# Sparse attention and an FFN on one core: x written by quarters, first-layer matmuls in halves at the block ends, more places for the first attention groups, named PSUM banks, new planner durations

## The chip, the cores and the metric

The kernel runs on one core of one Trainium2 chip. The time is the device time of one execution in microseconds (us); the kernel before has a median of 849.59 us over three runs (847.49 to 852.67). One execution was profiled.

The engines are called as the profile calls them: PE is the matmul engine (PEld its weight loads), DVE the vector engine, ACT the scalar engine, POOL the GpSimd engine, SP the engine that issues nearly all DMAs. PSUM is the memory that matmuls write to, SBUF the memory that all engines read.

## The reference

Attention over 8 batches of 8 heads, 576 tokens and 64 columns a head, followed by a two-layer feed-forward net on the 4608 resulting tokens:

```python
scores = q @ k.T / sqrt(64)            # per batch and head
mask_local   = (rel >= 0) & (rel < 32)               # heads 0 to 3; rel = query - key position
mask_strided = (rel >= 0) & (key % 32 == query % 32) # heads 4 to 7
attn = softmax(where(mask, scores, -1e9))
x = (attn @ v), heads side by side     # 4608 x 512
h = x @ w_in                           # 512 x 2048
out = (h * sigmoid(h)) @ w_out         # 2048 x 512
```

All is float32. The matmul operands of the net are split into a high part and a low part (`fp32r`), and each product is made of three matmuls: high by high, high by low, low by high.

## The kernel before, in words

**Attention.** Only the allowed pairs of queries and keys are computed. A batch is cut into six groups, three of local heads and three of strided heads; batch 0 runs group by group (units 0 to 5), the other batches in units of two groups (units 6 and up). A unit c passes these steps: `k` (DMA of queries and keys into one of three buffers `kd`), `S` (scores, PE, into a PSUM double bank), `M` (mask and row maximum, DVE, one pair of instructions per 128x64 piece), then for the first nine units `U` (subtraction on POOL) and `E` (one wide exponential on ACT), for later units one exponential with an accumulated sum per piece (`E c.j`, ACT), `R` (row sums and reciprocals, DVE), `N` (scaling, DVE), `T` (transposes, PE), `P` (copy from PSUM to a place `pt`, ACT), `v` (DMA of values), `O` (PE) and `B` (copy into `x`, ACT). In batch 0 the scores use the one double bank `pa`; transposes and `O` use the two double banks `po`.

**The net.** Tokens are worked in blocks of 512. Blocks 0 to 2 run directly: for each of 16 slices fc of the hidden width, the first layer is 12 matmuls 128x512 (`hidden`, L556 to L566; in block 0 as two halves `h` and `i` of six), then `t` (tanh, ACT), `g` (gate, DVE L577), `w` and `l` (high and low part of the result, DVE or ACT), then `o` (second layer, 12 matmuls, L610). A PSUM bank `ph` is given back by `g`; there are two. The weights are loaded in 32 pieces during block 0: `p` (DMA), `a` (two ACT instructions), `j` (DVE L333), `b` (high part, ACT or DVE), `d` (low part, DVE L373). The input of a block is split by `H` (high part, `x_high`, L551) and `L` (low part, `x_low`, L555), a step for each quarter cc of 128 columns of x; quarters 0 and 1 need the local heads, 2 and 3 the strided ones. The six remaining blocks run in three pairs with seven products in place of eight (steps `A`, L1325, and `B`, L1363; operands split by `hi` and `lo`; results by `rs` and stored by `st`). Meanwhile POOL forms sums of weights (`whole`, `sums`) for the pairs.

**The order.** Nothing is ordered by hand. Each step is an object of the class `Steps` with engines and costs, a due time, the steps that it follows and the rings of buffers that it takes from. `arrange` keeps a clock for each engine, picks among the steps that can start within `SOON` (0.05 us) of the earliest the one that is due first, and emits its instructions. Every engine then executes its own list strictly in that order, with waits on semaphores. So each changed cost, ring or dependence changes the lists of all engines.

**What the steps below touch.** In block 0 and in the step from block 0 to block 1, `x` is two tiles `xhi` and `xlo`; those of block 1 are new tiles in the same place, so that each of the eight steps `H1` and `L1` follows the last first-layer matmul of block 0, and the first matmul of block 1 follows all of them.

Of the kernel before, what the change touches and what calls it, by code (L numbers as in the profile page):

```python
# [106 lines left out]
SOON = 0.05  # L107

# [9 lines left out]
class Steps:  # L118
# [72 lines left out]
    def arrange(self):  # L191
# [18 lines left out]
        while len(order) < len(self.all):  # L210
# [11 lines left out]
            soon = [c for c in could if c[0] <= now + SOON]  # L222
# [18 lines left out]
def sparse_attention_ffn(ctx: ExitStack, tc: tile.TileContext, kqt, vt, w_in, w_out, out, out_t):  # L241
# [156 lines left out]
    class Attention:  # L398


        def __init__(self, b, gis):
# [71 lines left out]
        def scale(self):  # L473
            nc.vector.tensor_mul(self.s_sb, self.s_sb, self.inv)
# [8 lines left out]
        def turned(self, i):  # L483
            if i == 0:
                self.pt = att.tile([P, 7 * P], F32, name="pt", bufs=1)
            c0, n = self.c0[i] * P, self.gs[i].n * P
            nc.scalar.copy(out=self.pt[:, c0 : c0 + n], in_=self.psp[:, i, :n])
# [65 lines left out]
    def x_low(k, x, cc):  # L553
        for src, to in parts(k, cc):
            nc.vector.tensor_sub(out=x[1][:, cc, to], in0=src, in1=x[0][:, cc, to].bitcast(F32))  # L555
# [85 lines left out]
    def add_scores(c, t0=None):  # L641
# [4 lines left out]
        for g, gi, k in zip(a.gs, a.gis, a.k):  # L646
# [3 lines left out]
        s = do(f"S{c}", {"PE": 0.3 + sum(0.3 if g.local else 0.4 for g in a.gs)}, a.scores,  # L650
               reads=[f"kd{k}" for k in a.k], writes=[f"pss{c}"], takes=["pa"], due=after(0))
        ms = []
        for i, g in enumerate(a.gs):
# [931 lines left out]
```

## Time and profile before

| what | value |
|---|---|
| median of three runs | 849.59 us |
| profiled execution: its own time | 846.44 us |
| profiled execution: span from first to last instruction | 844.7 us |
| PE busy | 820.5 us (97%) |
| DVE, ACT, POOL busy | 529.5, 462.5, 117.6 us |
| DMA | 180.99 MB, mean 214 GB/s |

The time outside of the span is 1.74 us. The page's first part gives busy times, its second the span in 40 slices, its fourth the chain of waits that ended last; the timeline lists each engine's instructions in order of time with the idle time before them and what ended it in brackets; the view of stretches adds up each engine's busy time between given times.

### The profile page before, as it was taken

To read this page: it belongs to the slowest core of one execution; us is meant where nothing else is said; L and a number is where in the kernel's file an instruction comes from. 1 tells how busy PE (TensorE), PEld (TensorE's weight loads), DVE (VectorE), ACT (ScalarE), POOL (GpSimd) and SP (SyncE) were. 2 spreads that over 40 slices of the span, in tenths; PEclk is the share of its full clock that TensorE was granted. 3 is DMA by queue.
4 is the path that set the end of the run, shared out by engine and by line. 5 is a ranking of instruction groups with operands and counts; after the bars stand their busy time and mean duration, and the time that the engine had idled before them with its cause. 6 is when DMAs were issued, how large, how long until landed. Compare 5 with 4: busy or idle time off the path is not lost.

```text
span 844.7 us, 17679 instructions
## 1 busy us (share of the span) xinstructions
PE 820.5 (97%) x7040; PEld 669.1 (79%) x7040; DVE 529.5 (63%) x1257; ACT 462.5 (55%) x1051; POOL 117.6 (14%) x130
## 2 busy tenths in 40 slices
PE   5799998999999999999999999999999999999997
PEld 4588886788878888788888878888888888888886
DVE  5899777665575667712598675333886460289662
ACT  3888566545355545657596654565444344454440
POOL 4100003553563553000000000000000000000000
PEclk9999999999999999999999999999999999999999
DMA  7898885766655465656565856645456665555662
GB/s 263 287 312 265 244 257 199 242 213 229 208 169 162 146 221 175 225 209 246 193 245 201 265 212 250 231 163 194 161 197 222 225 248 191 183 188 187 211 235 99
DMA packets 76050, 180.99 MB, mean 214 GB/s; under 512 B 6336, under 2 KB 50368, under 8 KB 65216
## 3 DMA queue, kind: packets, MB, share of 16 engines
q1 hardware_dynamic: 75968, 179.87, 62.4%
q8 instruction: 55, 0.90, 0.4%
q14 instruction: 27, 0.22, 0.1%
HBM read 141.05 MB, written 38.80 MB: 213 GB/s over the span
## 4 chain that ended last, share of the span: by engine, by line
PE 89%; DVE 5%; DMA 2%; ACT 2%; issue 1%; POOL 1%; ACTq 0%; DVEq 0%; POOLq 0%
PE z L1325 27%; PE z L1363 26%; PE po L610 13%; PE ph L563 13%; PE pa L425 3%; PE pa L503 3%; PE pa L481 1%; DVE xlo L555 1%; PE po L503 1%; DMA w<-ops 1%; DMA stage<-w_out 1%; DMA ops<-stage 1%; PE po L481 1%; ACT sm L452 0%; DVE sm L443 0%
## 5 line engine op out<-in xcount | busy, mean ns | idle before, releaser
L1325 PE MATMUL z<-w,w 128*128 128x512 f32 x720 | 167.6, 391 | 0.5 <-DMA w<-ops 0.4
L1325 PEld LDWEIGHTS z<-w,w 128*128 128x128 f32 x720 | 134.3, 188 | 29.7 <-ACT w L1076 0.8
L1363 PE MATMUL z<-w,w 128*128 128x512 f32 x576 | 136.2, 391 | 0.0
L563 PE MATMUL ph<-xhi,w 128*128 128x512 f32 x384 | 132.2, 404 | 2.2 <-DVE th L577 2.1
L1363 PEld LDWEIGHTS z<-w,w 128*128 128x128 f32 x576 | 107.5, 188 | 22.6
L610 PE MATMUL po<-w,g 128*128 128x512 f32 x432 | 104.6, 391 | 0.1
L610 PEld LDWEIGHTS po<-w,g 128*128 128x128 f32 x432 | 80.7, 188 | 17.3 <-ACT osb L995 0.6
L452 ACT ACTIVATE sm<-sm,sums 128x64 f32<-128x64 f32 x240 | 80.1, 336 | 17.4 <-DVE sums L443 17.3
L563 PEld LDWEIGHTS ph<-xhi,w 128*128 128x128 f32 x384 | 72.6, 189 | 18.9 <-DVE th L577 3.0
L1195 DVE TENSOR_TENSOR w<-w,w 128x1024 fp32r<-128x1024 f32 (+3 forms) x68 | 77.7, 1151 | 13.5 <-ACT w L1266 11.0
L563 PE MATMUL ph<-xlo,w 128*128 128x512 f32 x192 | 75.6, 394 | 0.9 <-DVE xlo L555 0.9
L577 DVE SCALAR_TENSOR_TENSOR th<-th,ph 128x512 f32<-128x512 f32 x48 | 32.9, 686 | 51.3 <-ACT th L573 51.1
L1224 DVE TENSOR_TENSOR w<-w,z 128x1024 f32<-128x1024 f32 x30 | 36.6, 1219 | 39.2 <-PE z L1325 39.1
L1266 ACT CAST w<-w 128x1024 fp32r<-128x1024 f32 (+1 forms) x40 | 39.2, 987 | 35.1 <-PE z L1363 32.9
L573 ACT ACTIVATE th<-ph 128x512 f32<-128x512 f32 x48 | 28.5, 594 | 48.8 <-PE ph L563 43.0
L902 POOL TENSOR_TENSOR stage<-w,w 128x512 f32<-128x512 f32 x28 | 39.8, 1436 | 109.0 <-DMA ops<-stage 49.9
L1212 ACT ACTIVATE w<-w 128x1024 f32<-128x1024 f32 x30 | 31.8, 1061 | 37.2 <-DVE w L1224 36.9
L1363 PE MATMUL z<-xlo,w 128*128 128x512 f32 x216 | 52.1, 390 | 0.0
L1363 PE MATMUL z<-xhi,w 128*128 128x512 f32 x216 | 51.9, 389 | 0.0
L1218 ACT COPY w<-z 128x1024 f32<-128x1024 f32 x30 | 30.4, 1013 | 33.9 <-PE z L1325 33.9
L1363 PEld LDWEIGHTS z<-xhi,w 128*128 128x128 f32 x216 | 40.5, 188 | 8.4
L1363 PEld LDWEIGHTS z<-xlo,w 128*128 128x128 f32 x216 | 40.4, 188 | 8.4
(126 smaller groups left out, 1230.9 us busy)
## 6 DMA issues: line engine op xcount, KB each, us to landing
w<-ops SPq DMA_DIRECT2D x84, 1024.0 KB, 4.8
ops<-stage SPq DMA_DIRECT2D x48, 256.0 KB, 2.9
kd<-kqt SPq DMA_DIRECT2D x24, 448.0 KB, 5.2
ops<-w SPq DMA_DIRECT2D x80, 128.0 KB, 4.3
vd<-vt SPq DMA_DIRECT2D x24, 384.0 KB, 5.0
stage<-w_in SPq DMA_DIRECT2D x16, 512.0 KB, 5.2
stage<-w_out SPq DMA_DIRECT2D x16, 512.0 KB, 5.1
kd<-kqt SPq DMA_DIRECT2D x16, 442.0 KB, 5.3
```

The costliest lines, as they stand in the source:

```text
L452: nc.scalar.activation(out=self.s_sb[:, c, r], in_=self.s_sb[:, c, r], func=AF.Exp, bias=self.nmax[:, c, r : r + 1], scale=-1.0, accum_out ...
L503: nc.tensor.matmul(self.pso[to, b, at : at + wide], vds[v][half, tile_], self.pt[half, q0 : q0 + wide], start=True, stop=True,)
L563: nc.tensor.matmul(ph, weight(0, wi, fc)[:, cc * P : (cc + 1) * P], x[xi][:, cc], start=(cc, n) == (0, 0), stop=(cc, n) == (NP - 1, 2),)
L577: nc.vector.scalar_tensor_tensor(out=th[:, cols], in0=th[:, cols], scalar=1.0, in1=ph[:, cols], op0=ALU.add, op1=ALU.mult,)
L610: nc.tensor.matmul(po[tt], g[gi][:, cols], weight(1, wi, fc), start=fc == 0 and n == 0, stop=fc == NFC - 1 and n == 2,)
L902: nc.gpsimd.tensor_add(raw[:, 2 * n : 2 * n + 2].rearrange("p a q -> p (a q)"), weight(layer, 0, fc).bitcast(F32), weight(layer, 1, fc).bi ...
L1195: nc.vector.tensor_tensor(out=o, in0=x, in1=y, op=op1)
L1212: nc.scalar.activation(out=o, in_=x, func=AF.Silu)
L1224: nc.vector.tensor_add(o, x, y)
L1266: nc.scalar.copy(out=hi, in_=x)
L1325: nc.tensor.matmul(zt[z][:, jj], w[:, at, wi, cc * P : (cc + 1) * P], op[:, xi, cc], start=fresh and (cc, n) == (0, 0), stop=(cc, n) == (1 ...
L1363: nc.tensor.matmul(zt[zz][:, ds], w[:, at, wi, ds * P : (ds + 1) * P], op[:, gi, jj], start=fresh and (jp, jj, n) == (0, 0, 0), stop=(jp, ...
```

## The change

It does these things:

- **More places for batch 0.** A table `PLACES` says where each of the units 0 to 5 puts its scores, transposes and outputs, its `sm` tile and its `pt` tile: scores of units 1 and 3 go to a `po` bank, transposes of units 0 to 3 to the two small banks `ph`, and `osb` and `th` tiles serve as further `sm` and `pt` places.
- **Units 0 to 2 without POOL.** `U`, the wide `E` and the row-sum reduction now run only for units 3 to 8; units 0 to 2 use 18 exponentials of 128x64 with accumulated sums in place of three wide ones.
- **x by quarters.** `xhi` and `xlo` are one pair of tiles for blocks 0 to 2, and each quarter of them is a place of its own: `H` and `L` of a quarter follow only the matmuls that read this quarter. The low part may run on POOL, as may the scaling `N` of batches 0 and 1.
- **First layer in halves at the block ends.** In blocks 1 and 2 the slices 0 and 15 are two steps of six matmuls, `h` and `i`, as all slices of block 0 were before.
- **The last step in halves.** The last second-layer step of the last pair is made row half by row half, and its result is added and stored as two pieces of 256 KB in place of one of 512 KB.
- **Named double banks.** The pairs' three double banks are z0, z1, z2 with a name for each use, in place of a ring of three; the first three `A` steps each follow only the readers of the banks that lay there before.
- **The planner.** Nearly all costs are set anew, two PE steps in a row have no signal time between them, and until 34 us on the planner's clock the window of choice is 0.3 us in place of 0.05.

The core of the diff (costs that change by some hundredths are left out):

```diff
+PLACES = {
+    "pss": ("pa", "po", "pa", "po", "pa", "pa"),
+    "psp": ("ph", "ph", "ph", "ph", "po", "po"),
+    "pso": ("po",) * 6,
+    "sm": ("sm", "sm", "sm", "osb", "osb", "sm"),
+    "pt": ("pt", "th") * 3,
+}
+QUICK = (3, 4, 5)
...
+EARLY = 0.3
+FILLED = 34.0
...
                 far = SIGNAL if other.engine != "SP" else LANDING
+                if other.engine == "PE" and "PE" in step.costs:
+                    far = 0.0
...
-            soon = [c for c in could if c[0] <= now + SOON]
+            soon = [c for c in could if c[0] <= now + (EARLY if now < FILLED else SOON)]
...
-            self.quick = b < 2
+            self.quick = b == 1 or b == 0 and gis[0] in QUICK
+            self.sm_from = "sm" if b else PLACES["sm"][gis[0]]
+            self.pt_from = "pt" if b else PLACES["pt"][gis[0]]
+
+        def ring(self, name):
+            if self.b:
+                return "pa"
+            return PLACES[name][self.gis[0]]
...
-    def x_low(k, x, cc):
+    def x_low(k, x, cc, engine="DVE"):
+        sub = {"DVE": nc.vector, "POOL": nc.gpsimd}[engine].tensor_sub
         for src, to in parts(k, cc):
-            nc.vector.tensor_sub(out=x[1][:, cc, to], in0=src, in1=x[0][:, cc, to].bitcast(F32))
+            sub(out=x[1][:, cc, to], in0=src, in1=x[0][:, cc, to].bitcast(F32))
...
-        r = do(f"N{c}", {"DVE": 0.08 + 0.14 * a.n}, a.scale, reads=[f"sum{c}"], writes=parts,
+        costs = {"DVE": 0.08 + 0.14 * a.n}
+        if a.b < 2:
+            costs["POOL"] = 0.1 + 0.28 * a.n
+        r = do(f"N{c}", costs, lambda: a.scale(r.engine), reads=[f"sum{c}"], writes=parts,
...
+    def x_steps(k, cc, after=(), due=None):
+        more = 0.2 * (((k + 1) * T - 1) // S - k * T // S)
+        high = do(f"H{k}{cc}", {"ACT": 0.52 + more, "DVE": 0.5 + more},
+                  lambda: x_high(k, x, cc, high.engine), writes=[("x", cc)], after=after, due=due)
+        low = do(f"L{k}{cc}", {"DVE": 0.64 + 2.5 * more, "POOL": 1.5 + more},
+                 lambda: x_low(k, x, cc, low.engine), writes=[("x", cc)], due=due)
+        return high, low
...
-        ha = add(f"h{fc}", {"PE": 1.4}, due, [split_at[0, fc], lows[1]], first,
-                 takes=["ph"])
-        hb = add(f"i{fc}", {"PE": 1.4}, due, [ha, lows[3]], second)
+        ha = do(f"h{fc}", {"PE": 1.4}, first, reads=[("x", 0), ("x", 1)], after=[split_at[0, fc]],
+                takes=["ph"], due=due)
+        hb = do(f"i{fc}", {"PE": 1.4}, second, reads=[("x", 2), ("x", 3)], after=[ha], due=due)
...
-    x1 = new_x()
-    x_after = [made[-1][0]]
     for cc in range(NP):
-        x_steps(1, x1, cc, x_after + nexts, begin + pace * (NFC - 1))
+        x_steps(1, cc, nexts[cc // 2 :: 2], begin + pace * (NFC - 1))
...
+        halves = (range(NP // 2), range(NP // 2, NP)) if fc in (0, NFC - 1) else (range(NP),)
...
+            ring = {(SINGLE - 1, 2): "th", (SINGLE - 1, 3): "g"}.get((k, tt), "osb")
...
+        order = ("z0", "z1", "z2")[:: -1 if p % 2 else 1]
...
-                        for ds in range(2):
+                        for ds in range(2) if part is None else [part]:
...
+                        s = do(f"rs{p}.{i}.{ds}", {"DVE": 0.62}, half_go,
+                               reads=[("z", z[bank], ds), ("kept", p, base)],
+                               writes=[("res", p, i, ds)], takes=[] if ds else ["res"])
+                        do(f"st{p}.{i}.{ds}", {"SP": 1.0}, half_store, reads=[("res", p, i, ds)])
...
+    for name, before in (("A0.0.0", [f"t{last}.{NFC - 1}"]), ("A0.0.1", [f"q{last}.0", f"q{last}.1"]),
+                         ("A0.0.2", [f"q{last}.2", f"q{last}.3"])):
+        steps[name].after += [steps[s] for s in before]
```

Three places show what this does to the lists.

PE at the start, from the scores of unit 5 (`pa<-kd_84`) on, before the change. Rows into `po` from `ident` are transposes `T`, rows from `pt` outputs `O`, rows into `ph` from `xhi` the first half of the first layer, h0:

```order
L425 MATMUL pa<-kd_84 64x64 x12
L503 MATMUL po<-pt,vd_87 64x32 x24
L481 MATMUL po<-ident,sm 128x128 x4
L503 MATMUL po<-pt,vd_85 64x54 x16
L481 MATMUL po<-ident,sm 128x128 x4
L503 MATMUL po<-pt,vd_86 64x54 x16
L481 MATMUL po<-ident,sm 128x128 x3
L563 MATMUL ph<-xhi,w_0_507 128x512
```

and in the changed kernel, from the transposes of unit 3 on (`th` is now a `pt` place, `osb` an `sm` place):

```order
L506 MATMUL ph<-ident,osb 128x128 x4
L531 MATMUL po<-pt,vd_87 64x32 x24
L447 MATMUL pa<-kd_84 64x64 x12
L531 MATMUL po<-th,vd_85 64x54 x16
L506 MATMUL po<-ident,osb 128x128 x4
L592 MATMUL ph<-xhi,w_0_484 128x512
L592 MATMUL ph<-xlo,w_0_484 128x512
L592 MATMUL ph<-xhi,w_0_488 128x512
```

The first half h0, six matmuls, now stands ahead of O4 (outputs of unit 4, 64x54 from vd_86) and T5; before it stood behind both.

DVE a little later, from the low part of x's last quarter (L03, `xlo`) to the gate of slice 0 (g0, `th<-th,ph`), before the change; the score maxima of unit 6 stand ahead of it:

```order
L555 TENSOR_TENSOR xlo<-xb,xhi 128x512
L373 TENSOR_TENSOR w_0_520<-stage_522,w_0_507 128x512
L333 SCALAR_TENSOR_TENSOR stage<-stage 128x512 x2
L369 CAST w_0_575<-stage 128x512
L577 SCALAR_TENSOR_TENSOR th<-th,ph 128x512
```

and in the changed kernel, from the high part of that quarter (H03) on:

```order
L579 CAST xhi<-xb 128x512
L346 SCALAR_TENSOR_TENSOR stage_538<-stage_538 128x512
L584 TENSOR_TENSOR xlo<-xb,xhi 128x512
L382 CAST w_0_484<-stage_538 128x512
L346 SCALAR_TENSOR_TENSOR stage<-stage 128x512
L386 TENSOR_TENSOR w_0_488<-stage_538,w_0_484 128x512
L494 TENSOR_REDUCE sums<-sm 128x14
L495 TENSOR_SCALAR sums<-sums 128x14
L496 RECIPROCAL sums<-sums 128x14
L606 SCALAR_TENSOR_TENSOR th<-th,ph 128x512
```

H03 moved behind all maxima of unit 6, a weight step (j3) came between it and L03, and the row sums of unit 6 (R6) moved ahead of g0.

DVE at the end of block 0, before the change: the steps H10, H11, the gate g15, L10, L11 and then l15, the low part that the last second-layer step of block 0 reads (`g<-th,g`):

```order
L551 CAST xhi<-xb 128x64
L551 CAST xhi<-xb 128x448
...
L577 SCALAR_TENSOR_TENSOR th<-th,ph 128x512
L555 TENSOR_TENSOR xlo<-xb,xhi 128x64
L555 TENSOR_TENSOR xlo<-xb,xhi 128x448
...
L590 TENSOR_TENSOR g<-th,g 128x512
```

and in the changed kernel:

```order
L579 CAST xhi<-xb 128x64
L579 CAST xhi<-xb 128x448
L495 TENSOR_SCALAR sums<-sums 128x14
L496 RECIPROCAL sums<-sums 128x14
L584 TENSOR_TENSOR xlo<-xb,xhi 128x64
L584 TENSOR_TENSOR xlo<-xb,xhi 128x448
L606 SCALAR_TENSOR_TENSOR th<-th,ph 128x512
L499 TENSOR_TENSOR sm<-sm,sums 128x896
L619 TENSOR_TENSOR g<-th,g 128x512
```

Ahead of g15 and l15 there is now one quarter (H10 and L10) where there were two, with R9 and N9 of unit 9 in between; L11, L12 and L13 follow behind l15.

More of the change, by code (lines that the diff above doesn't have):

```diff
@@ L746, in piece_steps @@
                 lambda: high(i, h.engine), writes=lent_to)
-        d = add(f"d{i}", {"DVE": 0.62}, due + 1.5, [h], lambda: low(i))
+        d = add(f"d{i}", {"DVE": 0.66}, due + 1.5, [h], lambda: low(i))
         steps.reads(d, where)
@@ L751, in sparse_attention_ffn @@
     split_at = {pieces[i]: piece_steps(i) for i in range(len(pieces))}
-    def x_steps(k, x, cc, after, due):
-        high = add(f"H{k}{cc}", {"ACT": 0.52, "DVE": 0.47}, due, after,
-                   lambda: x_high(k, x, cc, high.engine))
-        return add(f"L{k}{cc}", {"DVE": 0.62}, due, [high], lambda: x_low(k, x, cc))
+    def x_steps(k, cc, after=(), due=None):
[5 more added lines that the diff above has]
+        return high, low
     done = (outs[:2], outs[1:3], outs[3:5], outs[4:6])
-    lows = [x_steps(0, x, cc, done[cc], 22 + cc) for cc in range(NP)]
+    lows = [x_steps(0, cc, done[cc], 22 + cc)[1] for cc in range(NP)]
     def chunk_steps(fc):
@@ L915, in go @@
             nc.gpsimd.tensor_sub(a12, a12, a11)
-        do(f"sums{layer}.{j}", {"POOL": 3.4}, go, writes=["raw0", "raw1"])
+        do(f"sums{layer}.{j}", {"POOL": 3.6}, go, writes=["raw0", "raw1"])
         for n in range(2):
@@ L1218, in go @@
                     nc.scalar.copy(out=o, in_=x)
[L1219 removed]
+            return do(f"cp{name}", {"ACT": 1.02}, go, reads=[zp], writes=[("G", g, jp)])
         def added(g):
@@ L1254, in mixed @@
         def mixed(o, x, y, add=False, times=1.0):
-            do(f"gm{name}{o}{x}{y}{add}", {"DVE": 1.12},
+            do(f"gm{name}{o}{x}{y}{add}", {"DVE": 1.17},
                lambda: g_mix(G[o, jp], G[x, jp], G[y, jp], add, times),
@@ L1338, in add_pair @@
                         if last:
-                            steps.ends(state["holder", z[jp]], "z", [end])
+                            steps.ends(state["holder", z[jp]], zt_name[z[jp]], [end])
                     add_unit(u + UNITS)
@@ L1461, in sparse_attention_ffn @@
             if fc == NFC - 1 and k + 1 < SINGLE:
-                nx = [None]
-                def fresh_x(nx=nx):
-                    nx[0] = new_x()
-                do(f"newx{k + 1}", {"POOL": 0.0}, fresh_x, after=[steps[f"h{k}.{fc}"]], writes=[("x", cc) for cc in range(NP)])
-                add_x(k + 1, nx, [steps[f"newx{k + 1}"]])
-                xk = nx
+                add_x(k + 1)
             if k == SINGLE - 1 and fc == NFC - 4:
```

199 lines of the change are left out of this document (114 added, 85 removed).

## The prediction

> **What bounds the kernel now.** I read the page's busy times first, then the chain of waits, then the stretches, to see where the bounding engine is idle.
>
> ```profile
> PE 820.5 (97%) x7040; PEld 669.1 (79%) x7040; DVE 529.5 (63%) x1257; ACT 462.5 (55%) x1051; POOL 117.6 (14%) x130
> PE 89%; DVE 5%; DMA 2%; ACT 2%; issue 1%; POOL 1%; ACTq 0%; DVEq 0%; POOLq 0%
> ```
>
> PE is busy for 820.5 of 844.7 us, and the change removes no matmul. So all it can win is the 24.2 us in which PE stands. The stretches (time, its length, busy time of each engine) say where these are:
>
> ```profile
> 0.00:4.21 4.21, 0.00 (x0) 0.00 (x0) 0.00 (x0) 1.28 (x1) 2.99 (x17) 1.00 0.55 180
> 4.21:28.33 24.12, 17.25 (x461) 14.53 (x461) 18.63 (x110) 12.38 (x25) 7.60 (x14) 1.00 0.85 279
> 28.33:43.78 15.45, 12.65 (x142) 9.41 (x141) 13.66 (x48) 13.09 (x26) 1.98 (x1) 1.00 0.83 296
> 43.78:130.00 86.22, 86.22 (x820) 70.60 (x819) 71.03 (x188) 62.42 (x134) 4.36 (x3) 1.00 0.86 271
> 130.00:142.00 12.00, 9.79 (x142) 7.35 (x140) 11.20 (x44) 4.97 (x21) 7.35 (x6) 1.00 0.41 137
> 236.00:250.00 14.00, 12.91 (x128) 9.51 (x130) 10.96 (x19) 6.55 (x15) 8.89 (x8) 1.00 0.43 144
> 330.00:345.00 15.00, 14.48 (x141) 11.47 (x140) 14.21 (x35) 7.41 (x19) 7.30 (x6) 1.00 0.54 191
> 345.00:839.60 494.60, 493.56 (x3327) 405.22 (x3325) 281.09 (x471) 262.88 (x482) 0.00 (x0) 1.00 0.59 209
> 839.60:844.70 5.10, 0.00 (x0) 0.00 (x0) 1.22 (x1) 0.00 (x0) 0.00 (x0) 0.70 0.26 103
> ```
>
> PE stands for 4.2 us until the first keys land, then 6.9 us up to h0 (24.12 less 17.25) and 2.8 us up to o0, the first second-layer step at 43.78; from there it never waits until 130. Block 0 ends with 2.2 us, block 1 with 1.1, block 2 with 0.5; the pairs lose 1.0 in 495 us, and behind the last matmul 5.1 us pass. The first 4.2 us and a last add and store stay whatever is done. The change touches all the rest.
>
> **The start: 0 (from -2.5 to +3.6).** Up to o0 both kernels do the same PE steps (units 0 to 5, h0 to h2, i0 to i2, scores of unit 6), so what counts is when o0 starts.
>
> ```profile
> 23.83 1.12 PE L503 MATMUL po<-pt,vd 64*64 64x54 f32 x32 [0.99 <-ACT pt L487]
> 24.88 1.11 PE L481 MATMUL po<-ident,sm 128*128 128x128 f32 x4
> 26.72 1.12 PE L503 MATMUL po<-pt,vd 64*64 64x54 f32 x32 [0.73 <-ACT pt L487]
> ```
>
> ```profile
> 28.67 2.56 PE ph L563 x6
> ...
> 70.94 2.72 PE ph L563 x12
> ```
>
> The second fence is of the chain of waits. O3 waited 0.99 for the single place `pt`; with two places this goes. T4 ended at 25.99, so now at about 25.0, and h0, which follows directly, starts there instead of at 28.33; the lighter steps of units 0 to 2 may give another 0.3, so 24.7. That is 3.6 us won. But the first six matmuls of 128x512 took 2.56 us where twelve took 2.72 later on: h0 runs cold. With h0 ahead of it, O4 starts at 24.7 + 2.56 = 27.3, against 26.72 before. Its copy B4 (0.95 us) was 28.41 to 29.36; now it is 28.4 to 29.3, the same. H02 waits for B4, and all of DVE's list waits behind H02.
>
> ```profile
> 28.41 0.95 ACT L532 COPY xb<-po 128x144 f32<-128x144 f32 x3
> 36.20 1.98 POOL L460 TENSOR_TENSOR sm<-sums,sm 128x896 f32<-128x896 f32 x1 [14.04 <-DVE sums L443]
> 35.95 0.69 DVE L555 TENSOR_TENSOR xlo<-xb,xhi 128x512 fp32r<-128x512 f32 x1
> 36.56 2.18 DVE L373 TENSOR_TENSOR w<-stage,w 128x512 fp32r<-128x512 f32 x1
> 40.20 0.68 DVE L577 SCALAR_TENSOR_TENSOR th<-th,ph 128x512 f32<-128x512 f32 x1
> 40.92 0.50 PE L563 MATMUL ph<-xhi,w 128*128 128x512 f32 x1 [2.12 <-DVE th L577]
> 41.73 1.07 DVE L469 TENSOR_REDUCE sums<-sm 128x14 f32<-128x896 f32 x1
> ```
>
> The wait that ends last here is that of h2 for g0, which gives its bank back. Before, U6 on POOL (36.20 to 38.18) held the weight step d3 on DVE: 2.18 us instead of 0.69. Now: H02 and L02 (0.4 and 0.6) until 30.4, j2, b2, d2 (0.6, 0.35, 0.6) until 31.9, the 14 maxima pairs of unit 6 (2.1) until 34.0, U6 on POOL from 34.15 to 36.15. Held by it are j3 and behind it L03, which ends at 37.4 against 36.64 before. Then b3, j4, d3 (1.55) and the row sums R6 (1.07 and two small ones, 1.45) stand ahead of g0: it starts at 40.4, against 40.20. So o0 comes where it was. All of h0's lead is lost in DVE's list. Ends: if U6 held nothing, 1.8 us would stay, and if h0's whole lead carried through, 3.6. If two more steps were held on this path (N0 behind U3, L01 behind U5; a `U` of three or four pieces took 1.20 us or less at 15.54, below), o0 would come 2.5 us later.
>
> ```profile
> 15.54 1.20 POOL L460 TENSOR_TENSOR sm<-sums,sm 128x512 f32<-128x512 f32 x1 [4.20 <-DVE sums L443]
> ```
>
> **End of block 0: 1.4 (0 to 2.2).**
>
> ```profile
> 129.28 2.90 PE L610 MATMUL po<-stage,g 128*128 128x512 f32 x12
> 136.40 2.56 PE L610 MATMUL po<-stage,g 128*128 128x512 f32 x10 [2.11 <-DVE g L590]
> 130.26 2.00 DVE L551 CAST xhi<-xb 128x64 fp32r<-128x64 f32 x4
> 132.18 0.67 DVE L577 SCALAR_TENSOR_TENSOR th<-th,ph 128x512 f32<-128x512 f32 x1
> 132.77 2.44 DVE L555 TENSOR_TENSOR xlo<-xb,xhi 128x64 fp32r<-128x64 f32 x4
> 135.14 1.21 DVE L590 TENSOR_TENSOR g<-th,g 128x512 fp32r<-128x512 f32 x1
> 136.27 2.49 DVE L555 TENSOR_TENSOR xlo<-xb,xhi 128x64 fp32r<-128x64 f32 x4
> ```
>
> The first layer of block 0 ends at 129.28; o14 and S10 take 4.0 us more, then o0.15 waits 2.11 for l15, which stood behind two quarters (4.44 us) on DVE; and block 1 starts when the last quarter ends, at 138.76, 9.5 us after 129.28. Now only H10 and L10 (1.0 and 1.22) stand ahead, and H10 may start after the first half h15, 1.36 us earlier; R9 and N9 (0.4 and 1.1) came in between. Counted from 129.28 with l14 done at about 0: H10 until 1.0, R9 1.4, L10 2.6, g15 3.3, N9 4.4, l15 5.1 to 5.6, so o0.15 waits 1.1 to 1.6 and h1.0 starts 0.7 earlier than before (T9, 0.7 us, moved behind it). With l14 done at -2.2 as before, l15 is done at 3.7, nothing waits, and 2.1 are won. I take the middle. L12 and L13 are hidden by h1.0, which no longer needs them.
>
> **End of block 1: 1.0 (0 to 1.1), of block 2: 0.2 (-0.5 to 0.5).**
>
> ```profile
> 245.23 0.73 PE L610 MATMUL po<-stage,g 128*128 128x512 f32 x2 [0.48 <-ACT g L586]
> 246.39 2.60 PE L610 MATMUL po<-stage,g 128*128 128x512 f32 x10 [0.42 <-DVE g L590]
> ```
>
> The two longest waits are for the high and the low part of g, which stand behind x on ACT and DVE. The halves give L20 and L21 1.36 us more, L22 and L23 the time of h2.0 and S15 as well, and g15 now stands behind two quarters instead of four. Block 2's 0.5 us belongs to operands of the pairs; its order barely moves.
>
> **The pairs: 0.7 (-0.5 to 1.0).**
>
> ```profile
> 504.50 1.39 PE L503 MATMUL pa<-pt,vd 64*64 64x32 f32 x80 [0.45 <-PE z L1363]
> 528.29 2.08 PE L1325 MATMUL z<-w,w 128*128 128x512 f32 x8 [0.40 <-DMA w<-ops]
> ```
>
> The 0.40 is for a weight unit whose place was read last by B0.5.3; that step now runs ahead of B0.6.0 and B0.6.1, two steps of 2.72 us earlier, so the load starts 5.4 us earlier. O23 and O24 also move by a step. The names z0 to z2 cost no instruction; a bad name would make PE wait for a copy of about 1.0 us, which I allow for once.
>
> **The end: 1.8 (1.2 to 2.2).**
>
> ```profile
> 839.60 1.22 DVE L1398 TENSOR_TENSOR stage<-z,g 128x1024 f32<-128x1024 f32 x1 [3.08 <-PE z L1363]
> 835.41 5.83 SPq L1401 DMA_DIRECT2D out_t<-stage  x2
> DMA to landing us min/median/max: 2.7/4.8/7.3
> DMA to landing us min/median/max: 2.0/2.5/4.4
> ```
>
> The first landing row is that of the results in pieces of 512 KB, the second that of block results in pieces of 256 KB. The last add ends at 840.82, the store follows, and the span ends 3.8 later. Now the first half is added under PE's last six matmuls, the second add takes 0.69 as 128x512 did elsewhere, and the store of 256 KB lands in 2.0 to 2.5: 0.5 and 1.3 are won.
>
> **The sum.** 0 + 1.4 + 1.0 + 0.2 + 0.7 + 1.8 = 5.1. The profiled execution took 846.44 (span 844.7 and 1.74 around it), so its like would take 841.3. It lies 3.15 below the median of the runs shown, so I forecast 849.6 - 5.1 = 844.5.
>
> [...]
>
> **Rivals.**
> (1) *The start keeps its lead.* For it: 3.6 us at h0, and units 0 to 2 lose three `U` and three reductions. Against: the list above. 844.5 - 3.0 = 841.5.
> (2) *DVE is held more often than counted*: N0 waits out U3, and L01 or d0 waits out U5 or L00. For it: the 2.18 of d3. Against: a hold costs only if DVE's list is then the last wait. 844.5 + 2.5 = 847.0.
> (3) *The last weight pieces stop PE: slower than before.* Pieces 24 to 31 pass through two places, and a31 now stands on ACT ahead of E9 and of the tanh of slice 14. Before, p31 was issued at 121.81 and a31 ran 5.4 us later. If d29, which frees the place, ends no earlier than before, a31 ends at 128.4, tanh, gate and l14 follow until 132.6, and o14, due at 128.2, waits 4.4 us; the 1.4 at this place go as well. 844.5 + 4.4 + 1.4 = 850.3. It decides from d29 ending after about 117 (each us later is one us). For it: ACT takes its list strictly in order. Against: d29 moves up, since it now follows j29 and b29 directly.
>
> ```profile
> 121.81 5.36 DMA stage<-w_out
> ```
>
> (4) *It does little*: the block ends wait as before for DVE, which has the same work, and only the last store is shorter: 849.6 - 2.0 = 847.6.
>
> **How the numbers follow.** Forecast 0.42, rival 1 0.17, rival 2 0.18, rival 3 0.09, rival 4 0.14. The forecast's own range is 842.5 to 846.5. Over the cases, with the bounds above and the 2 us or so by which medians of three runs differ, 840.0 to 850.0 holds 8 in 10. A measurement of this kernel tells about 1%, 8.5 us, from no change: faster than 841.1 is half of rival 1 and a tail of the forecast, 0.14; slower than 858.1 needs rival 3 and more, 0.03; within 1% 0.83.
>
> **What would show it.** Right: o0 within 2 us of 43.8 although h0 starts near 24.7 and is cold; j3 or L03 held under U6; PE's wait ahead of o0.15 under 1.6 us; none above 0.3 at the end of block 1; two last stores, and less than 3.6 us from the last matmul to the end. Wrong: o0 before 41.5 or after 46; a new wait above 1 us between 44 and 130, for d29, a31 or l14; new waits of `A` or `B` steps for a bank z0 to z2.

## The result and the profile after

The changed kernel takes 844.64 us (median of 10 runs, 842.19 to 845.92) beside 849.69 us for the kernel before on the same chip: a ratio of 0.9938, 95% interval 0.9919 to 0.9957. One of the ten runs of the kernel before took 3247.08 us; the ratio leaves it out. Timed again with six runs it took 842.74 beside 848.88, 0.9924 (0.9904 to 0.9943). All 16 runs together have a median of 843.7. The forecast of 844.5 holds, but largely by luck and not for the reasons that it gave: of its six terms one came out (the start), one had the wrong sign (the end of block 0), two were far off in size (the pairs, the end), and the two of blocks 1 and 2 were low.

The busy times and the chain of waits of the change's first profile (845.89 us, span 844.1):

```profile
PE 816.5 (97%) x7040; PEld 667.4 (79%) x7040; DVE 532.9 (63%) x1260; ACT 461.9 (55%) x1077; POOL 116.9 (14%) x129
PE 88%; DVE 6%; DMA 3%; ACT 1%; issue 1%; POOL 0%; DVEq 0%; ACTq 0%; SPq 0%; POOLq 0%
```

PE still bounds. The page looks as before, so I cut the span at the kernel's own milestones instead of at fixed times: the start of o0, of o14, the end of o0.15, of o2.15, and of the last matmul (o0.15 is the second-layer step of slice 15 in block 0; o0 and o14 are of block 0 too). The columns are time, length, busy time of PE, PEld, DVE, ACT and POOL, granted clock, DMA share and GB/s. The change:

```profile
4.33:44.80 40.47, 26.52 (x600) 20.11 (x601) 34.34 (x156) 29.15 (x82) 8.07 (x13) 0.92 0.85 293
44.80:130.34 85.54, 84.93 (x810) 69.27 (x808) 69.50 (x190) 57.66 (x125) 7.27 (x5) 1.00 0.84 264
130.34:141.19 10.85, 9.04 (x106) 6.81 (x105) 10.82 (x32) 6.55 (x23) 5.78 (x6) 0.84 0.55 189
141.19:353.97 212.78, 210.65 (x2308) 171.48 (x2308) 139.53 (x434) 111.51 (x396) 92.62 (x90) 1.00 0.59 194
353.97:839.37 485.40, 485.39 (x3222) 399.70 (x3220) 277.38 (x452) 255.75 (x453) 0.00 (x0) 1.00 0.59 210
839.37:844.09 4.72, 0.00 (x0) 0.00 (x0) 1.29 (x2) 0.00 (x0) 0.00 (x0) 1.00 0.29 111
```

The kernel before, cut in the same way (its first o0 starts at 43.78):

```profile
43.78:129.28 85.50, 85.50 (x816) 70.01 (x815) 70.35 (x187) 61.90 (x132) 4.36 (x3) 1.00 0.86 271
129.28:138.96 9.68, 7.47 (x106) 5.63 (x105) 9.65 (x19) 2.45 (x7) 7.35 (x6) 1.00 0.57 191
138.96:352.24 213.28, 211.29 (x2301) 170.26 (x2301) 140.50 (x447) 114.82 (x408) 93.30 (x90) 1.00 0.60 197
352.24:839.56 487.32, 486.32 (x3222) 399.31 (x3220) 275.53 (x450) 256.55 (x454) 0.00 (x0) 1.00 0.59 208
```

Two things stand out. The start and the end of block 0 became longer, not shorter (44.80 against 43.78, 10.85 against 9.68), at a granted clock of 0.92 and 0.84; and the pairs, of which I expected little, are where PE now never stands: 485.39 busy in 485.40.

These two profiles differ by 0.55 us only, though the medians differ by 5 to 6. The profile of before was a short run of its kernel (846.44, median 849.6), that of the change a long one (845.89, median 843.7). So both kernels were profiled again, below; the table has three profiles of each, and as won the difference of their means (before: executions of 846.44, 847.23 and 850.36 us; the change: 845.89, 844.36, and the 842.07 of the kernel with two tiles, which is the same program up to its last step).

| stage | before (three profiles) | change (three profiles) | won | predicted |
|---|---|---|---|---|
| up to o0 | 43.78, 43.44, 43.74 | 44.80, 43.55, 43.98 | -0.5 | 0 |
| o0 to o14 | 85.50, 85.82, 86.38 | 85.54, 85.29, 84.72 | 0.7, the length of T9, which moved on | - |
| o14 to end of o0.15 | 9.68, 9.14, 9.89 | 10.85, 11.69, 10.18 | -1.3 | 1.4 |
| to end of o2.15 | 213.28, 213.96, 214.04 | 212.78, 211.94, 211.91 | 1.6, with T9 (0.7) 2.3 | 1.2 |
| pairs | 487.32, 487.99, 489.43 | 485.40, 485.39, 485.39 | 2.9 | 0.7 |
| after the last matmul | 5.10, 5.11, 5.11 | 4.72, 4.72 | 0.4 | 1.8 |
| sum | 846.2 | 842.5 | 3.7 | 5.1 |

Three places of the change's trace carry the first three rows. At the start, its POOL, its DVE and PE's two waits (start, length, engine, line; idle time ahead and what ended it in brackets):

```profile
35.34 1.74 POOL L485 TENSOR_TENSOR sm<-sums,sm 128x896 f32<-128x896 f32 x1 [8.13 <-DVE sums L468]
35.45 2.18 DVE L346 SCALAR_TENSOR_TENSOR stage<-stage 128x512 int32<-128x512 int32 x1
37.55 0.68 DVE L584 TENSOR_TENSOR xlo<-xb,xhi 128x512 fp32r<-128x512 f32 x1
39.70 1.07 DVE L494 TENSOR_REDUCE sums<-sm 128x14 f32<-128x896 f32 x1
41.17 0.63 DVE L606 SCALAR_TENSOR_TENSOR th<-th,ph 128x512 f32<-128x512 f32 x1
35.59 0.80 PE L592 MATMUL ph<-xhi,w 128*128 128x512 f32 x1 [2.43 <-DVE xhi L579]
38.29 0.80 PE L592 MATMUL ph<-xlo,w 128*128 128x512 f32 x1 [1.90 <-DVE xlo L584]
44.80 1.52 PE L639 MATMUL po<-w,g 128*128 128x512 f32 x6
```

From U6 on this is what was forecast, step by step and within 1.0 us: U6 holds j3 (2.18 us where the same instruction took 0.68 at 38.49), behind it L03, R6 stands ahead of g0, and h0's lead (24.48) is gone at o0. One step ahead of it is not: h0 was forecast cold (2.56 us of work), and isn't (2.03). Its matmuls, first of the change, then of before:

```profile
24.80 0.40 PE L592 MATMUL ph<-xlo,w 128*128 128x512 f32 x1
26.58 0.50 PE L592 MATMUL ph<-xlo,w 128*128 128x512 f32 x1 [0.73 <-DVE xlo L584]
```

```profile
28.90 0.63 PE L563 MATMUL ph<-xlo,w 128*128 128x512 f32 x1
```

They take 0.40 where they took 0.63; in place of the longer matmuls, PE waits 0.73 for L01. New is also that PE's waits of 2.43 and 1.90 halved its clock (0.50 granted), as the fillers below show. The same at the end of block 0; the stretches here are those in which the granted clock was low, first of the change, then of a variant without them (the fillers, below):

```profile
35.24:42.07 6.83, 4.58 (x10) 2.99 (x11) 6.76 (x11) 4.72 (x8) 1.74 (x1) 0.50 0.64 235
137.64:141.05 3.41, 3.41 (x10) 2.67 (x9) 3.41 (x20) 2.39 (x12) 0.00 (x0) 0.50 0.45 160
```

```profile
35.24:42.07 6.83, 4.86 (x20) 3.73 (x21) 6.68 (x12) 5.90 (x11) 0.56 (x1) 1.00 0.67 236
137.64:141.05 3.41, 3.41 (x17) 2.82 (x16) 3.41 (x28) 2.31 (x14) 0.00 (x0) 1.00 0.60 210
```

In the same 6.83 us PE finished 10 matmuls at half clock and 20 at full (six of the 20 are repeats that the variant puts in), in the 3.41 us 10 and 17, none of them a repeat. At the end of block 0 the cause stands on POOL and DVE (the change):

```profile
129.10 2.87 POOL L935 TENSOR_TENSOR stage<-w,w 128x512 f32<-128x512 f32 x2 [4.10 <-DMA ops<-w]
129.49 2.74 DVE L579 CAST xhi<-xb 128x64 fp32r<-128x64 f32 x2
133.05 1.20 DVE L584 TENSOR_TENSOR xlo<-xb,xhi 128x64 fp32r<-128x64 f32 x2
135.77 1.22 DVE L619 TENSOR_TENSOR g<-th,g 128x512 fp32r<-128x512 f32 x1
135.55 0.73 PE L639 MATMUL po<-stage,g 128*128 128x512 f32 x2 [1.05 <-ACT g L615]
137.04 4.14 PE L639 MATMUL po<-stage,g 128*128 128x512 f32 x10 [0.76 <-DVE g L619]
```

POOL's first additions for the pairs' weight sums run while H10 (the high part of block 1's first quarter) stands on DVE: its two casts, 128x64 and 128x448, take 0.49 us where POOL is free (below), and 2.74 here and in the second profile of the change. L10, g15, N9 and l15 follow, o0.15 waits 1.05 and 0.76, and its last ten matmuls take 4.14 where they took 2.56 before.

### The profile page after: what moved, and what is told of

It is laid out like the page before. It is cut to its first block, busy times and chain, and to the rows that moved or that the text cites. A ratio compares the mean times of both kernels' runs of the same rounds, so it can differ in the third digit from the quotient of the medians.

```text
span 844.1 us, 17715 instructions
## 1 busy us (share of the span) xinstructions
PE 816.5 (97%) x7040; PEld 667.4 (79%) x7040; DVE 532.9 (63%) x1260; ACT 461.9 (55%) x1077; POOL 116.9 (14%) x129
## 4 chain that ended last, share of the span: by engine, by line
PE 88%; DVE 6%; DMA 3%; ACT 1%; issue 1%; POOL 0%; DVEq 0%; ACTq 0%; SPq 0%; POOLq 0%
PE z L1374 27%; PE z L1413 27%; PE ph L592 13%; PE po L639 13%; PE pa L531 3%; PE pa L447 3%; PE pa L506 2%; DMA stage<-w_in 2%; DMA kd<-kqt 1%; DVE xhi L579 1%; DVE stage L346 1%; DMA stage<-w_out 1%; DVE xlo L584 1%; DVE w L386 1%; DVE sm L499 0%
## 5 line engine op out<-in xcount | busy, mean ns | idle before, releaser
L477 ACT ACTIVATE sm<-sm,sums 128x64 f32<-128x64 f32 x258 | 86.1, 337 | 28.5 <-DVE sums L468 28.3
L935 POOL TENSOR_TENSOR stage<-w,w 128x512 f32<-128x512 f32 x28 | 37.0, 1340 | 109.8 <-DMA ops<-stage 100.4
L477 ACT ACTIVATION_READ_ACCUMULATOR sm<-sm,sums 128x1 f32 x258 | 48.8, 189 | 0.0
```

Of the source, the lines that this page charges most:

```text
L477: nc.scalar.activation(out=self.s_sb[:, c, r], in_=self.s_sb[:, c, r], func=AF.Exp, bias=self.nmax[:, c, r : r + 1], scale=-1.0, accum_out ...
L935: nc.gpsimd.tensor_add(raw[:, 2 * n : 2 * n + 2].rearrange("p a q -> p (a q)"), weight(layer, 0, fc).bitcast(F32), weight(layer, 1, fc).bi ...
```

## The experiments

**What does the usual run of before look like, and has the clock a part in it?** Kernel before, unchanged.

> The kernel before, unchanged, profiled and timed once more, to learn what its usual execution looks like. Its one profile had a granted clock of 0.998 and 846.44 us, while its median is 849.7. Theory A (waits only): the clock is as high in its other runs, 0.997 or more, and the 3 us between profile and median come from longer waits of PE. Theory B (clock): in the usual run the clock is halved for one or more stretches of 3.4 us after a wait of PE, as in the profile of the change; then its runs show 0.992 to 0.996, and those with the lower clock are the longer ones, by about 1.7 us for each stretch.

Median of 12 runs 849.53 (846.30 to 852.69). The profiled run took 847.23, with two halvings of the clock (25.7 to 29.1, 39.4 to 42.8). Neither theory holds whole: the granted clock of its runs lies between 0.992 and 0.999, but it doesn't order them (0.999 at 847.82 and 848.46, 0.998 at 851.0, 0.995 at 846.30). What lengthens the run of before stays open here; the third profile, below, shows a part of it.

**The start undone.**

```diff
-    "pss": ("pa", "po", "pa", "po", "pa", "pa"),
-    "psp": ("ph", "ph", "ph", "ph", "po", "po"),
...
+    "pss": ("pa",) * 6,
+    "psp": ("po",) * 6,
...
-    "sm": ("sm", "sm", "sm", "osb", "osb", "sm"),
-    "pt": ("pt", "th") * 3,
+    "sm": ("sm",) * 6,
+    "pt": ("pt",) * 6,
 }
-QUICK = (3, 4, 5)
+QUICK = (0, 1, 2, 3, 4, 5)
...
-EARLY = 0.3
+EARLY = 0.05
```

> The change without its places for batch 0: scores, transposes, sm and pt of units 0 to 5 in the places of before, POOL's subtraction and the wide exponential in all six units, one window of choice. The prediction gave the start as 0 (-2.5 to +3.6): 844.6 within 1 us, o0 near 43.8. The rival reads the profile of the change, where o0 came at 44.8 and the clock was halved from 35.2 to 42.1: the new places cost, and without them o0 comes at 43 to 44, the clock stays full after it first opens, and the median falls to 842 to 843.5.

842.79 (840.88 to 844.55; 0.9923, 0.9901 to 0.9945). h0 starts at 30.47, 6 us later than in the change, and o0 at 43.52, no later: the lead in h0 is worth nothing at o0, as forecast. In the profiled run the clock was halved in other stretches (19.4 to 29.6, 149.1 to 152.5), so that part of the rival fails there, though three of the six runs show 0.998 or more. The edit also changed the order at the end of block 0: o0.15 has no wait, but PE waits 3.46 for a gate step ahead of 149.60. Its median lies in the rival's range, but it can't be told from the change's own 842.74 and 844.64.

**PE kept busy in its waits.**

```diff
         for cc in ccs:
             for n, (wi, xi) in enumerate(((0, 0), (0, 1), (1, 0))):
+                if (fc, cc) == (0, 3) and n < 2 and first_x and 1 in FILL:
+                    again(3 if n == 0 else 0)
+                    again(6)
+                    if n:
+                        first_x.clear()
...
+                if (k, fc, tt) == (0, NFC - 1, 0) and n != 1 and 2 in FILL:
+                    if spare is None:
+                        spare = ps.tile([P, T], F32, name="ph")
+                    for m in range(3):
+                        nc.tensor.matmul(
+                            spare, weight(0, 0, fc)[:, :P], state["g", fc - 1][0],
+                            start=m == 0, stop=m == 2,
+                        )
```

(`again(n)` repeats the first n of the six matmuls of h1 into h1's own bank; `FILL` is `(1, 2)`, so both places are on.)

> The change, with 21 more matmuls of 128x512 put into waits of PE: 9 ahead of the wait for H03 and 6 ahead of the wait for L03 in i0 (they repeat the six of h1 into the bank of h1), and 3 and 3 ahead of the two waits in o0.15 (into a free bank). They take about 4.8 us of PE, in waits of 2.43, 1.90, 1.05 and 0.76. Theory B (the clock is halved because PE stands too long): both halvings, 35.2 to 42.1 and 137.6 to 141.1, go; the clock is 0.997 or more; the work in these stretches takes about half the time, 3.4 to 3.6 us less than in the profiled 845.9, and all runs lie at 841.5 to 843. Theory A: the clock has no part in it; the median stays at 844.6 or rises by up to 0.5.

842.00 (840.64 to 843.25; 0.9914, 0.9891 to 0.9937), six runs with a granted clock of 0.999 or 1.0, against 0.992 to 0.996 in all 16 of the change. So here it was PE's waits that halved the clock, and matmuls that compute nothing new kept it full. It is worth about 1.7 us against the 843.7 of all runs of the change, though the intervals of the ratios overlap, and not the expected 3.4 to 3.6, since only one of the two places pays: at the end of block 0 the ten matmuls take 2.58 again (4.14), while o0 came at 43.76, for PE then waits for g0 instead:

```profile
36.14 0.50 PE L606 MATMUL ph<-xhi,w 128*128 128x512 f32 x1 [2.15 <-DVE xhi L580]
40.90 0.50 PE L606 MATMUL ph<-xhi,w 128*128 128x512 f32 x1 [1.07 <-DVE th L621]
```

**The end: two tiles.**

```diff
+                        if (p, i) == (PAIRS - 1, 6):
+                            zt[zz] = Halves(zt[zz], pools["ps2"].tile([P, 2, T], F32, name=order[2]))
```

> The change, with the two halves of the last result in two PSUM tiles (two double banks) in place of the two halves of one. The prediction had the first half added under the last six matmuls, and 1.8 us won at the end; in the profile of the change the two adds ran back to back behind the last matmul, 4.7 us before the end (5.1 before). If the cause is that the first add waits for all writes of its tile: now it starts about 1.3 us before the last matmul ends, and 3.6 to 4.1 us pass from the last matmul to the end. If it waits for something else (its place of the store, the kept sum): no difference, 4.7. The median moves by 0.6 to 1.0 or by nothing.

843.06 (841.80 to 845.60; 0.9929, 0.9907 to 0.9951). DVE and PE at the end, of the change and then of this kernel, whose last matmul ends at 836.18:

```profile
839.40 1.29 DVE L1464 TENSOR_TENSOR stage<-z,g 128x512 f32<-128x512 f32 x2 [8.52 <-PE z L1413]
```

```profile
834.86 0.69 DVE L1475 TENSOR_TENSOR stage<-z,g 128x512 f32<-128x512 f32 x1 [7.17 <-PE z L1423]
836.22 0.69 DVE L1475 TENSOR_TENSOR stage<-z,g 128x512 f32<-128x512 f32 x1 [0.67 <-PE z L1423]
```

In the change both adds start behind the last matmul (839.37) and take 1.29, no less than the one add of before (1.22). The wait is set for the tile, not for its half: with a tile for each half the first add runs 1.3 us ahead of the end, and 4.08 us pass from the last matmul to the end instead of 4.72. The median can't tell 0.6 from nothing.

**The change once more, as the measure of the next three.**

> The changed kernel, unchanged, once more, as the measure for the three runs beside it and for a second profile. Median 844.6 (842 to 846). The first profile had two halvings of the clock (35.2 to 42.1 and 137.6 to 141.1) and o0 at 44.8; the kernel with two tiles, whose order is the same up to the end, had one (35.0 to 41.8) and o0 at 44.0. Expected here: one to three halvings, o0 at 43.8 to 44.8, PE without a wait from 354 to the last matmul, 485.4 us.

842.74 (840.58 to 844.36). The profile has o0 at 43.55, halvings at 33.8 to 40.7 and 136.2 to 139.6 (and a mean granted clock of 0.92 from 4.33 to 24.5), and pairs of 485.39.

**One line of the planner undone.**

```diff
-                if other.engine == "PE" and "PE" in step.costs:
-                    far = 0.0
```

> The change without one line of the planner: two PE steps in a row have a signal time between them again, as before. The traces so far have the pairs (from the end of o2.15 to the last matmul) at 487.3 and 488.0 us in two profiles of before and at 485.4 in four of the change and its variants. Theory: what won there is PE's order, which this line sets: of the 87 rows in which PE's order of steps differs from before, 82 go back with it, all 10 of the first pair among them. Then the pairs take 486.5 to 488.0 again and the median is 1 to 3 above after_again. Rival: the names of the double banks, or the new costs of ACT's and DVE's steps, won it: 485.4 stays, and the median within 0.7.

845.76 (845.04 to 846.56; 0.9960, 0.9944 to 0.9976): 3.0 us above the change beside it. The size fits the theory, the place does not. The pairs take 485.88, 0.5 more and not 1 to 2.6. In its profile (846.02, 1.7 above that of the change beside it) the largest new loss is a wait of 1.71 in block 0 (transposes behind their scaling on DVE, at 97.66); from the end of o0.15 to that of o2.15 PE stands for 2.74 us (1.30), but ahead of o0.15 for only 0.65 (2.77). So PE's order in the pairs is not what won the most there, and where the 3.0 of the medians arises is not fully placed.

**Unit 6 without POOL.**

```diff
-            self.quick = b == 1 or b == 0 and gis[0] in QUICK
+            self.quick = b == 1 and gis[0] > 0 or b == 0 and gis[0] in QUICK
```

> The change with unit 6 done like units 0 to 2: no subtraction on POOL, seven exponentials with accumulated sums on ACT in place of one wide one, no reduction R6 of 1.07 on DVE. Theory of the prediction: U6 held j3 and L03 on DVE (2.10 for j3), and R6 stood ahead of g0, so that h0's lead was lost; without them L03 ends about 1.4 us earlier, g0 starts at 39.0 to 40.0 in place of 41.2, and o0 at 41.8 to 43.0; the wait of PE for L03 falls from 1.9 to under 1, and the median falls by 1 to 3. Rival: ACT, which now has 4.8 us of exponentials ahead of the tanh t0, becomes the last wait: o0 at 43.5 to 46, no gain.

837.84 (836.88 to 838.35; 0.9865, 0.9846 to 0.9885), 4.9 below the change beside it. Its DVE and PE at the place of the fence on the start:

```profile
34.28 0.68 DVE L346 SCALAR_TENSOR_TENSOR stage<-stage 128x512 int32<-128x512 int32 x1
34.89 0.68 DVE L584 TENSOR_TENSOR xlo<-xb,xhi 128x512 fp32r<-128x512 f32 x1
38.29 0.69 DVE L606 SCALAR_TENSOR_TENSOR th<-th,ph 128x512 f32<-128x512 f32 x1 [0.24 <-ACT th L602]
35.62 0.50 PE L592 MATMUL ph<-xlo,w 128*128 128x512 f32 x1 [0.71 <-DVE xlo L584]
```

j3 takes 0.68, L03 ends at 35.6 (38.2), g0 starts at 38.29 (41.17), o0 at 42.24: the theory's path, with o0 in its range and L03 and g0 earlier than it said. The rival had a part: g0 now waits 0.24 for ACT. At o0 the edit wins 1.3 us (43.55 beside it); the larger share comes later, where the planner's order turned over too: h1.0 stands ahead of o0.15, PE has no wait from 40 until o1.15 ends at 241.9, and from o14 to the end of o2.15 218.4 us pass instead of 223.6. The edit also takes R6's reduction (1.07) off the way to g0, and this run doesn't part the shares of POOL, of R6 and of the order.

**Whole first-layer steps at the block ends.**

```diff
-        halves = (range(NP // 2), range(NP // 2, NP)) if fc in (0, NFC - 1) else (range(NP),)
+        halves = (range(NP // 2), range(NP // 2, NP)) if False else (range(NP),)
```

> The change with slices 0 and 15 of blocks 1 and 2 as whole steps of 12 matmuls, as before, instead of halves. The prediction gave the ends of blocks 1 and 2 1.2 us, from the halves and from x by quarters. If the halves do it: the waits at these two places grow from 1.1 and 1.0 to 2 or more and the median rises by 1 to 2. If they do nothing, because S12 waits there for a copy on ACT and g for DVE as before: waits and median the same within 0.5.

841.10 (839.68 to 843.03; 0.9908, 0.9888 to 0.9928): not slower, so the halves of blocks 1 and 2 win nothing; the interval overlaps that of the change. In its profile PE waits 0.95 in block 1 and not at all in block 2, no more than in the change's first profile (1.11 and 1.02). Its end of block 0 has another order, though, and takes 8.1 us, so the lower median is not the halves' alone.

**POOL's additions held back.**

```diff
-               writes=[f"raw{n}"], after=[split_at[layer, fc]])
+               writes=[f"raw{n}"], after=[split_at[layer, fc], *(steps[f"L1{cc}"] for cc in range(NP))])
```

> The change, with POOL's preparation of the weight sums (additions of two 128x512 operands) held back until the four quarters of x of block 1 are done. In three profiles of the change's order the first of these additions ran at 128.4 to 132.0, over H10 on DVE, whose four casts then took 2.66 us; from the start of o14 to the end of o0.15 10.2 to 11.7 us passed, against 9.7 and 9.1 in two profiles of before, and the clock was halved there in two of the three. Theory: POOL's additions hold H10 and L10, and so g15 and l15, for which o0.15 waits. Without them H10 takes about 1 us, h1.0 can go ahead of o0.15, PE stands under 0.7 there and the clock stays full; with the start as in the change (o0 43.5 to 44.9) the median falls by 2 to 5, to 838.5 to 841.5. Rival: H10 and L10 are late because l14 is (129.6), not because they are held, and L11 and L12 on POOL hold DVE as well; waits of 1.5 or more stay, and the median is within 1 of 843.7.

839.98 (838.03 to 841.46; 0.9898, 0.9880 to 0.9915), the theory's range. DVE and POOL in its profile, and the stretches from o14 to o0.15 and on to o2.15:

```profile
128.94 0.49 DVE L579 CAST xhi<-xb 128x64 fp32r<-128x64 f32 x2
129.96 4.65 POOL L584 TENSOR_TENSOR xlo<-xb,xhi 128x64 fp32r<-128x64 f32 x4 [5.81 <-ACT xhi L579]
134.57 2.92 POOL L935 TENSOR_TENSOR stage<-w,w 128x512 f32<-128x512 f32 x2
```

```profile
129.12:139.89 10.77, 10.16 (x119) 7.83 (x118) 8.86 (x39) 6.82 (x33) 9.55 (x9) 1.00 0.80 263
139.89:348.04 208.15, 207.83 (x2297) 169.22 (x2295) 140.72 (x416) 111.37 (x391) 97.32 (x96) 1.00 0.60 194
```

H10 takes 0.49 in place of 2.74. As POOL is free, the planner gives it L11 and L12, and moves h1.0 and i1.0 ahead of o0.15 (119 matmuls in the stretch instead of 106). Both stretches together last 218.9 us; in the change 223.6 (222.1 in the profile with two tiles). How much of the 4.7 is the hold and how much the order that follows from it, this run doesn't part.

**Three edits together** (unit 6, whole steps, two tiles).

> Three edits of the runs before together: unit 6 without POOL's subtraction (837.8 alone), whole first-layer steps at the ends of blocks 1 and 2 (841.1 alone), the last result in two tiles (0.6 at the end). If the three places are separate, 837.8 less 0.6 and less up to 2: 835.5 to 837.5. If the gain of whole steps was the end of block 0, which unit 6's edit wins already: 837.0 to 838.

838.16 (837.79 to 840.10; 0.9880, 0.9866 to 0.9894): no better than unit 6's edit alone. The second guess was nearer.

**One ring of double banks again.**

```diff
-        order = ("z0", "z1", "z2")[:: -1 if p % 2 else 1]
+        order = ("z", "z", "z")
...
-    steps.rings.update({"z0": 1, "z1": 1, "z2": 1, "res": 2})
+    steps.rings.update({"z": 3, "res": 2})
...
-        steps[name].after += [steps[s] for s in before]
+        pass
```

> The change with one ring of three double banks again instead of three named ones, and the first three A steps without their added followers; the order of PE's steps stays the same. Six profiles with the named banks have the pairs at 485.4 us, two of before at 487.3 and 488.0, the one without the planner's line at 485.9. If the names win what is left: 486.5 or more. If they win nothing and the rest comes from the order and from operands that are ready earlier: 485.4.

```profile
352.37:837.76 485.39, 485.39 (x3221) 399.50 (x3220) 277.36 (x452) 255.80 (x453) 0.00 (x0) 1.00 0.59 210
```

485.39 for the pairs, what the change has within 0.01: the names win nothing there. One run, 844.26.

**The kernel before a third time.**

> The kernel before a third time, for its profile alone. Two profiles took 846.4 and 847.2 while the median of 39 runs is about 849. If this one lies near 849 or above, its stages say where the usual run is longer: at the start (o0 at 43.4 and 43.8 so far), at the end of block 0 (clock halved or not), or ahead of the pairs, where PE waited 0.8 for an operand from ACT in the second profile and not in the first. If it lies near 847 again, that stays open.

850.36, and the stages say where in part: of the 3.9 above the first profile, its pairs take 2.1 (489.43). PE's waits in them, and what ACT did ahead of the first:

```profile
360.55 11.18 PE L1325 MATMUL z<-w,w 128*128 128x512 f32 x48 [1.06 <-ACT w L1218]
507.42 1.39 PE L503 MATMUL pa<-pt,vd 64*64 64x32 f32 x80 [0.45 <-PE z L1363]
514.66 2.97 PE L1363 MATMUL z<-w,w 128*128 128x512 f32 x12 [0.17 <-DMA w<-ops]
531.66 16.61 PE L1325 MATMUL z<-w,w 128*128 128x512 f32 x72 [0.43 <-DMA w<-ops]
690.79 16.60 PE L1325 MATMUL z<-w,w 128*128 128x512 f32 x72 [0.60 <-DMA w<-ops]
```

```profile
358.38 1.22 ACT L995 ACTIVATE osb<-po 128x512 f32<-128x512 f32 x2 [2.58 <-DMA out<-osb]
359.49 1.92 ACT L1218 COPY w<-z 128x1024 f32<-128x1024 f32 x2
```

The first wait begins with block 2's results: ACT's copies into `osb` wait 2.58 us for the store that still reads one of the two `osb` places, and the copy that PE waits for stands behind them. The 0.45 ends with PE's own matmuls and is the same in all three profiles; the others wait for weight units from DRAM. All but the 0.45 hang on when a DMA lands: 0, 0.83 and 1.06 us for the first, 0.54, 0.15 and 1.20 for the weight units in the three profiles (all waits of the pairs: 1.0, 1.43 and 2.71). The change's ACT at this place waits for no store (its `osb` rows have no wait ahead), as the third and fourth result go to a `th` and a `g` place:

```profile
352.65 1.09 ACT L1041 ACTIVATE osb<-po 128x512 f32<-128x512 f32 x2
354.01 0.60 ACT L1041 ACTIVATE th<-po 128x512 f32<-128x512 f32 x1 [0.27 <-PE po L639]
```

## Why the prediction was right, and where it was wrong

**The start (0 predicted, -0.5 measured): right, by its own steps on DVE.** h0 at 24.48 (24.7 said), O4 at 27.2 (27.3), U6 over j3, L03 at 38.2 (37.4), g0 at 41.2 (40.4), o0 at 44.80, 43.55 and 43.98 (43.8). Undoing the places left o0 at 43.52; taking U6 away moved it to 42.24. One step of it was wrong: h0 was not cold (save its first matmul in the profile with two tiles). Its 2.56 us came out as 2.76 by luck, 2.03 of work and the wait of 0.73 for L01; in the two other profiles h0 took 2.40 and 1.89. Not foreseen were the halved clock, and two more holds on DVE: in the first profile a weight cast took 1.39 us beside L00 on POOL (0.43 elsewhere), a step j 1.33 beside U3 (0.69). What these two cost at o0, no run shows.

**The end of block 0 (+1.4 predicted, -1.3 measured): wrong in sign.** The order of the list was right, and l14 was late as in the first of its two cases (129.6, 0.8 ahead of o14). Two steps of the sum failed. H10 was put at 1.0; under POOL's additions it took 2.74 (0.49 in the run that holds them back), so that l15 ended 6.6 us after the start of o14, not 5.1 to 5.6, and the waits came to 1.81, 2.77 and 2.71 (before 2.21, 1.73 and 2.42). And the cost of a wait was counted as its length; here it also halved the clock in two of three profiles, 1.6 and 1.4 us more on ten matmuls (4.14 and 4.00, against 2.58). The stretch of before stood in the prediction with POOL busy for 7.35 of 12 us, and H10's 2.00 for four casts was quoted: the hold was there to be read.

**Blocks 1 and 2 (1.2 predicted, 2.3 measured): size low, and not by the step named.** The halves win nothing (whole steps were no slower). In block 1 the waits for g fell away, and a new one took their place, scores of unit 12 behind a copy on ACT, which stands behind the cast w15, which waits for g15:

```profile
246.05 1.35 PE L447 MATMUL pa<-kd 64*32 64x64 f32 x80 [1.11 <-ACT pt L515]
```

```profile
244.62 0.62 ACT L615 CAST g<-th 128x512 fp32r<-128x512 f32 x1 [2.60 <-DVE th L606]
245.14 0.85 ACT L515 COPY pt<-pa 128x384 f32<-128x384 f32 x2
```

PE's idle time in this whole stage is 2.13, 1.30 and 1.28 in the change and 1.99, 2.64 and 3.06 before, 1.0 less on average; the rest of the 2.3 is not placed. The sign named for this place, no wait above 0.3 at the end of block 1, did not come: 1.11, 0.78 and 0.76.

**The pairs (0.7 predicted, 2.9 measured): the term that was mis-sized most.** I priced the waits of one profile, 1.0 us, and took that for the stage. Most of them hang on DMAs, and they vary: 1.0, 1.43 and 2.71, 1.7 on average. The other 1.1 of the 2.9 is not idle time: PE's busy time in the pairs fell from 486.32, 486.55 and 486.72 to 485.39. Part of that goes with the waits (72 matmuls behind a wait take 16.6 us above, 16.48 in the change without one); the rest is not placed. The change and its variants have none in ten profiles, 485.4 each time; only without the planner's line 0.23 came back. This also moves the median against the profile: the 3.15 by which the first profile lay below its median was carried over to the change as if it belonged to the chip; part of it belonged to these waits. So it is luck that the sum of 5.1, made against one profile, fits the medians (5 to 6) better than the profiles' own 3.7. What removed the waits is settled in part: not the bank names (485.39 without them), 0.5 by the planner's line; the places for block 2's results were read off the trace, not tried alone, and for the weight units the cause stays open.

**The end (1.8 predicted, 0.4 measured).** The first step failed: the first half is not added under the last six matmuls, since its wait is for the whole tile. The second was too large: from the end of the last add to the end of the span 3.84 us became 3.40, not 2.5. The store landed 2.0 us after its issue where it took 2.7, but 1.1 of the 3.84 lay outside the landing, and there 1.4 remained; the forecast had counted it as landing.

**The rivals.** Rival 1 (lead kept) fell at o0. Rival 2 (DVE held more often) happened in its mechanism, at H10 (2.74 us) and at the two weight steps of the start (1.39 and 1.33) rather than at N0 or L01, and the pairs made up for it. Rival 3 (late weight pieces) came half: d29 ended at 118.7, past its point of 117, and l14 came 2.5 us later than before, but o14 did not wait; what it cost by pushing H10 back was not measured apart. Rival 4 (little but the last store, 847.6) fell with the pairs, though it was right that the block ends still wait for DVE. So the total came out right by luck: against the forecast the end of block 0 lost 2.7 us and the end 1.4, the pairs won 2.2 and blocks 1 and 2 1.1.

## What to carry to other kernels

Profile both kernels more than once before pricing waits of a tenth to one us: here the same wait took 0, 0.83 and 1.06 us in three profiles. A wait of PE can cost more than its length, here 1.8 us of waits and 1.6 of halved clock behind them, so work that can stand ahead of the waiting step (h1.0 ahead of o0.15) can be worth more than the wait. And where POOL's long instructions hold DVE (here j3 took 2.18 us beside U6 and 0.68 without it), keep them out of the stretch in which DVE's list is the last wait: unit 6 taken off POOL, its reduction on DVE with it, won 1.3 us at o0, and 4.9 in all with the order that followed from it.

## What the runs showed of the hardware

The clock was halved for stretches of 3.41, 6.83 and (19.4 to 29.6, with the start undone) 10.2 us, multiples of one length, and in the change after waits shorter than it: 2.43 and 1.90 us with 0.8 of work between, and 1.05 and 0.76 with 0.7 between. Two variants have waits longer than it: 3.46 and 3.62 us with the start undone, 4.2 without the planner's line. With the same order at the end of block 0, the clock was halved there in two profiles (from 137.6 us behind 1.81 of waits, from 136.2 behind 2.77) and not in a third (2.71, two tiles). So the length of the waits alone does not settle it here; what else does, no run tests.

The clock that the profile gives does not show every stretch of long matmuls. In the first profile of before it is given as 1.00 from the start up to 839.6, yet the matmuls of 128x512 take 0.63 us until 31, as long as in the halved stretch of the change (39.73, 41.01), and 0.39 to 0.40 from 33.8; in the first profile of the change they take 0.40 from 24.8. So a run's mean clock, such as the 0.998 of that profile of before, leaves this stretch out.
